# Second products in blocks of seven for two of three token groups, and weight sums made in the first group

## The chip, the core and the metric

The kernel runs on one core of a Trainium2 chip. The core has five engines with queues of their own, each worked through in order: TensorE (PE, matrix products into PSUM), VectorE (DVE), ScalarE (ACT), GpSimd (POOL, cannot reach PSUM) and SyncE (SP), which here issues nearly all DMA transfers. The metric is the device time of one launch in microseconds (us); the kernel before takes 1295.29 us (median of three runs, 1294.5 to 1299.32).

## The reference, cut to what matters

```python
# q, k, v: [4, 8, 576, 64]
attn = softmax(q_c @ k_c.T / sqrt(64)) @ v_c          # in chunks of 64 positions
x = attn, rearranged to [2304, 512]
h = maximum(x @ w_in, 0);  x = h * h @ w_out          # first layer: 512 -> 2048 -> 512
p = domain_probs / (domain_probs.sum(-1, keepdims=True) + 1e-9)
for e in range(4):                                    # second layer: four experts
    h = maximum(x @ w1[e], 0)                         # 512 -> 1024
    out += p[:, e:e+1] * (h @ w2[e])                  # 1024 -> 512
```

All of it is float32. The kernel writes each operand as a high part (rounded for the fast matmul) and a low part (the rest), and makes three matmuls (high-high, high-low, low-high) for each product.

## The kernel before

**First layer.** Attention and the first layer run in ticks r = 0 to 85. The 2304 tokens are five blocks of 384, 384, 512, 512 and 512; the 2048 hidden features are four passes of four groups of 128. So the first layer has 80 steps, 20 in a pass: 8 of 384 tokens and 12 of 512. Step m runs in tick r = m + 5. A tick has twelve matmuls of l1 (first matrix, L298) for step m, then twelve of l2 (second matrix, L331) for step m - 1. Between them ScalarE takes the relu (L309), VectorE squares (L310), ScalarE makes the high part (L314), VectorE the low part (L315); the l2 of the next tick reads these. From tick 22 on attention is over. The first layer's weights come as 64-bit numbers; each of 32 units is converted (unit_convert, unit_split: ScalarE L129, L130, L151, four steps of VectorE, GpSimd L143, L144, L152) in a tick that UOFF and SECOND give: in the third pass at ticks 26, 28, 30, 33 and 41 to 44, in the fourth at 46, 48, 50, 53 and 61 to 64.

**Jobs.** The second layer's products are made with seven block products in place of eight (a Strassen form), which needs sums of weight blocks. A job takes one of 16 pieces (four experts, four chunks of 256 hidden features) of one of the two weights: it loads the blocks (job_load, three DMAs), makes four sums on GpSimd (L470), splits the seven blocks in four parts into high and low (ScalarE L477 for the high part, then GpSimd or VectorE L479 for the low one) and stores them to DRAM (kept, L484). There are 32 jobs, one every second tick from tick 20 on, interleaved with the first layer: loaded in tick r, summed in r + 2, split from half a tick later on. The split tile jsplit has three buffers, jraw three.

**Second layer.** The tokens are three groups of 768 (six tiles of 128: three of a top half, three of a bottom half). Each group has 16 steps, numbered n = 0 to 47 in all. A step has seven slots u. In slot u stands one product of the first kind for step n (c_unit, L529: six matmuls of 384 columns), and, for steps whose first product is finished, three products of the second kind (d_unit, L610: nine matmuls of 256 columns). c_finish turns the first products into the blocks A11, A12, A22 and the sums S1 to S4 (VectorE L547, L541; GpSimd L578; ScalarE L551 and GpSimd L552 split them). d_move takes the second products out of PSUM: B and A collect into the tile uw, O, x1, x0, o1, o0 scale by the probability of the expert and add to the output tile, F adds uw at the end of an expert (j == 3); B at an expert's first step (j == 0) is a copy on ScalarE (L627). At every step w1_load and w2_load bring the stored sums back (1792 KB each). The output has six tiles of one buffer each.

The order on each engine is the order in which this code issues; there is no scheduler.

Of the kernel before, what the change touches and what calls it, by code (L numbers as in the profile page):

```python
# [18 lines left out]
P = 128  # L19
# [17 lines left out]
JOB_AT, JOB_EVERY = 20, 2  # L37
# [7 lines left out]
def tile_kernel(ctx, tc, q, k, v, moe_w_in, moe_w_out, moe2_p, moe2_w1, moe2_w2, out):  # L45
# [395 lines left out]
    def job_load(which, n):  # L441
        e, j = divmod(n, NP)
        r = late["jb"].tile([P, 7, 2 * P], F32, tag="raw", name="jraw", bufs=3)
        if which == 1:
            for i, h0, h1, slot in ((0, 0, 2, 1), (1, 0, 1, 0), (1, 1, 2, 3)):
                f0 = (2 * j + i) * P
                nc.sync.dma_start(
                    out=r[:, slot:slot + h1 - h0].rearrange("p h (k f) -> p (h k) f", k=2),
                    in_=moe2_w1[e, h0 * 2 * P:h1 * 2 * P, f0:f0 + P].rearrange("(k p) f -> p k f", p=P),
                )  # L450
        else:
            f0 = 2 * j * P
# [12 lines left out]
    def job(which, n):

        r = job_load(which, n)
        yield 4
        for o, a, b, op in SUMS[which]:
            nc.gpsimd.tensor_tensor(out=r[:, o], in0=r[:, a], in1=r[:, b], op=op)  # L470
        yield 3
        c = NW // 4
        done = []
        for part in range(4):
            x = r.rearrange("p s c -> p (s c)")[:, part * c:(part + 1) * c]
            w = late["jb"].tile([P, 2, c], F32R, tag="split", name="jsplit", bufs=3)
# [3 lines left out]
            done.append((kept[which, n][:, :, part * c:(part + 1) * c], w.bitcast(F32)))  # L480
# [437 lines left out]
```

## Time and profile before

| | |
|---|---|
| median of three runs | 1295.29 us |
| the profiled execution | 1293.79 us, of which 1292.0 us are the span of the trace |
| TensorE, weight loads | 1217.7 us (94%), 1133.6 us (88%) |
| VectorE, ScalarE, GpSimd | 67%, 50%, 60% busy |
| granted TensorE clock, mean | 0.974 of full speed |

Busy means that an instruction was being executed, at whatever clock; waits are shown beside the instruction that came after them, with what ended them.

### The profile page before, as it was taken

What the parts mean: (1) busy time and instruction counts of PE and PEld (TensorE: products, weight loads), DVE (VectorE), ACT (ScalarE), POOL (GpSimd) and SP (SyncE); (2) the same over time, 40 slices, a digit from 0 to 9 for tenths busy, and PEclk for the clock granted to TensorE, in tenths of its full rate; (3) what the DMA queues carried; (4) which work ended last, traced back from release to release, by engine and by line L of the source; (5) the groups of instructions that cost most, each with busy time, mean ns of one, the idle gap of its engine ahead of it and who ended that gap; (6) DMA issues with size and microseconds to landing.
All of it is one profiled execution on the core that took longest, in us unless ns stands there. A gap on an engine that the chain in (4) does not pass through costs nothing.

```text
span 1292.0 us, 22549 instructions
## 1 busy us (share of the span) xinstructions
PE 1217.7 (94%) x8344; PEld 1133.6 (88%) x8344; DVE 866.3 (67%) x1437; ACT 641.6 (50%) x1335; POOL 773.5 (60%) x773
## 2 busy tenths in 40 slices
PE   7899997898799899989999999999999999999997
PEld 6798886776677788879999999899999989999996
DVE  6965774457655746646767677676767766767676
ACT  5655554444444444544545456545444564545453
POOL 3500278667765865835676668476756675656665
PEclk7999998999999899999999999999999999999999
DMA  9854136685659388586666666766665686666562
GB/s 205 194 119 122 43 91 206 216 289 181 218 197 302 133 290 278 205 330 265 259 256 229 229 239 257 269 263 254 251 228 229 245 302 229 259 263 235 228 229 106
DMA packets 152381, 288.81 MB, mean 224 GB/s; under 512 B 66000, under 2 KB 127440, under 8 KB 146128
## 3 DMA queue, kind: packets, MB, share of 16 engines
q1 hardware_dynamic: 149648, 286.72, 64.0%
q8 instruction: 65, 1.06, 0.3%
q10 hardware_dynamic: 2624, 0.66, 0.2%
q14 instruction: 44, 0.36, 0.1%
HBM read 223.91 MB, written 63.44 MB: 222 GB/s over the span
## 4 chain that ended last, share of the span: by engine, by line
PE 73%; DMA 8%; DVE 6%; ACT 4%; POOL 4%; issue 3%; SPq 2%; DVEq 0%; ACTq 0%; POOLq 0%
PE psa L610 25%; PE pst L529 21%; PE psa L331 10%; PE pst L298 5%; PE psh L298 4%; PE psh L529 4%; DMA w2d<-jsplit 3%; DMA w1d<-jsplit 2%; POOL jsplit L479 2%; DMA q<-in_q 1%; PE pst L274 1%; POOL raw L143 1%; DMA k<-in_k 1%; ACT jsplit L477 1%; PE pst L218 1%
## 5 line engine op out<-in xcount | busy, mean ns | idle before, releaser
L529 PE MATMUL pst<-ar 128*128 128x384 f32 x1728 | 349.1, 337 | 4.6 <-ACT u L559 3.7
L529 PEld LDWEIGHTS pst<-ar 128*128 128x128 f32 x1728 | 291.0, 189 | 5.4 <-ACT u L559 4.1
L331 PE MATMUL psa<-ar 128*128 128x512 f32 (+1 forms) x960 | 238.1, 392 | 37.1 <-ACT ar L314 34.1
L552 POOL TENSOR_TENSOR ar<-s,ar 128x384 fp32r<-128x384 f32 x192 | 194.7, 1025 | 107.0 <-ACT ar L551 102.3
L331 PEld LDWEIGHTS psa<-ar 128*128 128x128 f32 x960 | 182.5, 198 | 73.9 <-ACT ar L314 39.7
L610 PE MATMUL psa<-ar 128*128 128x256 f32 x1512 | 212.7, 284 | 12.4 <-ACT uw L627 8.9
L610 PEld LDWEIGHTS psa<-ar 128*128 128x128 f32 x1512 | 201.0, 188 | 19.5 <-ACT uw L627 12.6
L610 PE MATMUL psa<-w2x,ar 128*128 128x256 f32 x1512 | 202.0, 278 | 0.6 <-DVE uw L629 0.4
L610 PEld LDWEIGHTS psa<-w2x,ar 128*128 128x128 f32 x1512 | 195.7, 188 | 2.3 <-DVE uw L629 0.6
L643 POOL TENSOR_TENSOR o<-o,x 128x256 f32<-128x256 f32 x135 | 106.6, 790 | 100.7 <-ACT x L639 100.6
L551 ACT CAST ar<-s 128x384 fp32r<-128x384 f32 x192 | 98.5, 513 | 91.0 <-DVE s L547 85.9
L631 DVE TENSOR_TENSOR uw<-psa,uw 128x512 f32<-128x512 f32 x144 | 95.1, 687 | 66.7 <-ACT uw L627 31.7
L143 POOL TENSOR_TENSOR raw<-raw 128x512 f32<-128x512 f32 x32 | 35.1, 1098 | 173.5 <-DVE raw L142 84.1
L479 DVE TENSOR_TENSOR jsplit<-jraw,jsplit 128x448 fp32r<-128x448 f32 x64 | 56.4, 881 | 110.1 <-ACT jsplit L477 102.1
L298 PE MATMUL pst<-ar 128*128 128x512 f32 (+1 forms) x576 | 129.7, 375 | 0.0
L477 ACT CAST jsplit<-jraw 128x448 fp32r<-128x448 f32 x128 | 71.0, 567 | 106.7 <-DMA w1d<-jsplit 46.3
L298 PEld LDWEIGHTS pst<-ar 128*128 128x128 f32 x576 | 108.5, 193 | 14.5
L559 ACT COPY u<-pst 128x384 f32<-128x384 f32 x144 | 69.9, 486 | 91.5 <-PE pst L529 88.1
L629 DVE TENSOR_TENSOR uw<-psa,uw 128x512 f32<-128x512 f32 x108 | 74.6, 691 | 55.6 <-PE psa L610 55.2
L479 POOL TENSOR_TENSOR jsplit<-jraw,jsplit 128x448 fp32r<-128x448 f32 x64 | 77.5, 1211 | 56.0 <-ACT jsplit L477 48.4
L570 ACT ACTIVATE ar<-psh 128x384 fp32r<-128x384 f32 x96 | 47.3, 492 | 124.4 <-DVE psh L566 66.2
L470 POOL TENSOR_TENSOR jraw<-jraw 128x256 f32<-128x256 f32 x128 | 105.9, 848 | 2.5
(118 smaller groups left out, 1811.5 us busy)
## 6 DMA issues: line engine op xcount, KB each, us to landing
ar<-w1d SPq DMA_DIRECT2D x48, 1792.0 KB, 7.5
ar<-w2d SPq DMA_DIRECT2D x48, 896.0 KB, 7.8
w2x<-w2d SPq DMA_DIRECT2D x48, 896.0 KB, 7.5
w1d<-jsplit SPq DMA_DIRECT2D x64, 448.0 KB, 3.8
w2d<-jsplit SPq DMA_DIRECT2D x64, 448.0 KB, 3.6
raw<-in_moe_w_in SPq DMA_DIRECT2D x16, 512.0 KB, 5.3
raw<-in_moe_w_out SPq DMA_DIRECT2D x16, 512.0 KB, 5.5
jraw<-in_moe_w SPq DMA_DIRECT2D x32, 256.0 KB, 4.3
```

The costliest lines, as they stand in the source:

```text
L298: nc.tensor.matmul(ph[:, :T], lhsT=w[:, kk, :], rhs=x[tb][:, kk, :], start=(kk == 0 and n == 0), stop=(kk == KD - 1 and n == 2),)
L331: nc.tensor.matmul(o, lhsT=w, rhs=y, start=(f == 0 and n == 0), stop=(f == G - 1 and n == 2))
L470: nc.gpsimd.tensor_tensor(out=r[:, o], in0=r[:, a], in1=r[:, b], op=op)
L477: nc.scalar.copy(w[:, 0], x)
L479: eng.tensor_tensor(out=w[:, 1], in0=x, in1=w[:, 0].bitcast(F32), op=ALU.subtract)
L529: nc.tensor.matmul(p, lhsT=w[:, kk, :], rhs=y[:, kk, :], start=(kk == 0 and z == 0 and u in (0, 1, 3)), stop=(kk == 1 and z == 2 and u in ...
L551: nc.scalar.copy(h, st[n, nm])
L552: nc.gpsimd.tensor_tensor(out=l, in0=st[n, nm], in1=h.bitcast(F32), op=ALU.subtract)
L610: nc.tensor.matmul(p, lhsT=w, rhs=y, start=(k in (1, 7) and z == 0), stop=(k in (3, 4) and z == 2), skip_group_check=True,)
L629: nc.vector.tensor_tensor(out=uw, in0=b, in1=uw, op=ALU.add)
L631: nc.vector.tensor_tensor(out=uw, in0=pb[n, t, 0], in1=uw, op=ALU.add)
L643: nc.gpsimd.tensor_tensor(out=o1[:, :2 * P], in0=o1[:, :2 * P], in1=x, op=ALU.add)
```

## The change

The second products of group 1 (steps n = 0 to 15) are made plainly: plain_unit makes six matmuls of 512 columns for each of the six token tiles, plain_move adds them to the output tile. Groups 2 and 3 keep the seven-block form. The second weight's sums are still made by jobs beside the first layer, 16 of them, in the ticks of the new list JOBS, with jsplit in four buffers and jraw in two. The first weight's sums are made in group 1 itself: w1_raw loads a piece two or three steps ahead, w1_add makes the four sums on GpSimd, w1_split writes high and low parts straight to the place from which the matmuls read, and w1_keep stores them for groups 2 and 3. w2_raw and w2_split bring the plain second weight. What the first two steps need is done in ticks 67 to 81 (early), in a pool that takes the place of the first layer's weight buffers. There are eight output buffers; B of the third tile at j == 0 goes to VectorE; the last step has an order of its own (LAST).

```diff
-JOB_AT, JOB_EVERY = 20, 2
+JOBS = [23, 26, 29, 32, 35, 44, 47, 50, 53, 56, 64, 67, 70, 73, 76, 79]
+SWAP = 67
...
+    def job(n):
...
+        r = late["jb"].tile([P, 7, 2 * P], F32, tag="raw", name="jraw", bufs=2)
...
         yield 4
-        for o, a, b, op in SUMS[which]:
-            nc.gpsimd.tensor_tensor(out=r[:, o], in0=r[:, a], in1=r[:, b], op=op)
-        yield 3
+        for o, a, b in ((4, 0, 1), (5, 3, 4), (0, 0, 3), (6, 2, 5)):
+            nc.gpsimd.tensor_tensor(out=r[:, o], in0=r[:, a], in1=r[:, b], op=ALU.subtract)
+        yield 2
...
-            w = late["jb"].tile([P, 2, c], F32R, tag="split", name="jsplit", bufs=3)
+            w = late["jb"].tile([P, 2, c], F32R, tag="split", name="jsplit", bufs=4)
...
+    def w1_add(n, part):
+        r = raw1[n]
...
+        nc.gpsimd.tensor_tensor(out=r[:, o], in0=r[:, a], in1=r[:, b], op=op)
...
+    def w1_split(n, part):
+        c = NW // 2
+        if part == 0:
+            w1_slot(n)
+        h, l = (y[:, part * c:(part + 1) * c] for y in w1c[n])
+        a = raw1[n].rearrange("p s k f -> p (s k f)")[:, 2 * P + part * c:2 * P + (part + 1) * c]
+        nc.scalar.copy(h, a)
+        nc.gpsimd.tensor_tensor(out=l, in0=a, in1=h.bitcast(F32), op=ALU.subtract)
+
+    def w1_keep(n):
+        nc.sync.dma_start(out=kept[1, n].rearrange("p z c -> p (z c)"), in_=w1_slot(n))
+
+    def w2_split(n, part):
...
+        nc.scalar.copy(h, a)
+        nc.gpsimd.tensor_tensor(out=l, in0=a, in1=h.bitcast(F32), op=ALU.subtract)
...
         elif at == 5:
             nc.vector.tensor_tensor(out=d, in0=d, in1=st[n, "u2"], op=ALU.add)
+            if plain(n):
+                nc.scalar.activation(out=g[n][A21][0], in_=d, func=AF.Relu)
+                return
...
+        elif at == 6 and plain(n):
+            low(n, A21, d)
+            nc.scalar.activation(out=g[n][A12][0], in_=b, func=AF.Relu)
...
+    def plain_unit(n, t):
...
+        for i in range(2):
+            hi, lo = g[n][((A11, A21), (A12, A22))[i][tau]]
+            for z, (w, y) in enumerate(((hi, bh), (hi, bl), (lo, bh))):
+                nc.tensor.matmul(
+                    p, lhsT=w[:, ts], rhs=y[:, i, :], start=(i == 0 and z == 0), stop=(i == 1 and z == 2)
+                )
+
+    def plain_move(n, t):
...
+        if m == 0:
+            nc.scalar.activation(out=o, in_=p, func=AF.Copy, scale=pe)
+        else:
+            nc.vector.scalar_tensor_tensor(out=o, in0=p, scalar=pe, in1=o, op0=ALU.mult, op1=ALU.add)
...
             b = pb[n, t, 1]
-            if j == 0:
+            if j == 0 and t == 2:
+                nc.vector.tensor_copy(out=uw, in_=b)
+            elif j == 0:
                 nc.scalar.copy(uw, b)
...
+    LAST = {
+        1: ((0, "B"),), 2: ((1, "B"),), 3: ((0, "A"), (0, "W"), (1, "A"), (1, "W"), (0, "x1"), (0, "o1")),
+        4: ((0, "F"), (0, "D1"), (1, "x1"), (1, "o1"), (0, "O"), (0, "D0")),
+        5: ((1, "F"), (1, "D1"), (1, "x0"), (1, "o0"), (1, "D0")),
+        6: ((2, "B"), (2, "A"), (2, "W"), (2, "F")), 7: ((2, "X"), (2, "D1"), (2, "O"), (2, "D0")),
+    }
...
+        early = {
+            SWAP: [(w1_raw, (0,)), (w1_raw, (1,)), (w2_raw, (0,))],
+            LEAD + NS - 4: [(w1_split, (0, 0)), (w1_split, (0, 1)), (w1_raw, (2,))],
+        }
...
+                if u in (0, 1) and n + 1 < NU:
+                    w1_split(n + 1, u)
+                if u == 1 and n < NU:
+                    w1_keep(n)
+                    if n + 3 < NU:
+                        w1_raw(n + 3)
+                if u in (2, 3) and n < NU:
+                    w2_split(n, u - 2)
+                if u == 3 and n + 1 < NU:
+                    w2_raw(n + 1)
+                if u >= 3 and n + 2 < NU:
+                    w1_add(n + 2, u - 3)
+                if 0 < n <= NU and u < 6:
+                    t = (u + 3) % 6
+                    plain_unit(n - 1, t)
+                    plain_move(n - 1, t)
```

Where the change moves instructions, the programs of before and after read as follows. First ScalarE in the ticks of the conversion cluster of the third pass (ticks 41 to 43); line numbers of the changed kernel are one higher here, and its job copy is L461. Before:

```order
L314 CAST ar<-pst 128x512
L129 ACTIVATE cv<-raw 128x512
L130 ACTIVATE raw<-raw 128x512
L477 CAST jsplit<-jraw 128x448 x2
L309 ACTIVATE r<-pst 128x512
L314 CAST ar<-pst 128x512
L129 ACTIVATE cv<-raw 128x512
L130 ACTIVATE raw<-raw 128x512
L151 CAST ar<-cv 128x512
L477 CAST jsplit<-jraw 128x448 x2
L309 ACTIVATE r<-pst 128x512
```

and after:

```order
L315 CAST ar<-pst 128x512
L130 ACTIVATE cv<-raw 128x512
L131 ACTIVATE raw<-raw 128x512
L310 ACTIVATE r<-pst 128x512
L315 CAST ar<-pst 128x512
L130 ACTIVATE cv<-raw 128x512
L131 ACTIVATE raw<-raw 128x512
L152 CAST ar<-cv 128x512
L310 ACTIVATE r<-pst 128x512
```

The pair of job copies that stood between the conversion and the relu of the next tick is gone from these ticks.

TensorE where the first layer ends and the second begins (L298 and L331 are l1 and l2, L529 the first product, L610 the second; after: L299, L332, L562, and L674 is plain_unit). Before:

```order
L298 MATMUL psh<-ar 128x512 x12
L331 MATMUL psa<-ar 128x512 x12
L529 MATMUL pst<-ar 128x384 x6
L331 MATMUL psa<-ar 128x512 x12
L529 MATMUL psh<-ar 128x384 x6
L529 MATMUL pst<-ar 128x384 x36
L529 MATMUL psh<-ar 128x384 x6
L610 MATMUL psa<-ar 128x256 x9
```

and after:

```order
L299 MATMUL psh<-ar 128x512 x12
L332 MATMUL psa<-ar 128x512 x12
L562 MATMUL pst<-ar 128x384 x6
L332 MATMUL psa<-ar 128x512 x12
L562 MATMUL psh<-ar 128x384 x6
L562 MATMUL pst<-ar 128x384 x36
L674 MATMUL psa<-ar 128x512 x6
L562 MATMUL psh<-ar 128x384 x6
```

The second product of step 0 begins one slot earlier, and a slot has six matmuls of 512 columns where it had nine of 256.

GpSimd in one step of group 1 (s are the sums S1 to S4, x the scaled products, raw the weight pieces). Before:

```order
L643 TENSOR_TENSOR o<-o,x_5826 128x256
L643 TENSOR_TENSOR o<-o,x_5850 128x256
L578 TENSOR_TENSOR s_5865<-s_5861,a_5768 128x384
L552 TENSOR_TENSOR ar<-s_5863,ar 128x384
L552 TENSOR_TENSOR ar<-s_5865,ar 128x384
L552 TENSOR_TENSOR ar<-s_5861,ar 128x384
L643 TENSOR_TENSOR o<-o,x_5925 128x256
L552 TENSOR_TENSOR ar<-s_5913,ar 128x384
L651 TENSOR_TENSOR o<-o,x_5927 128x512
```

and after, two steps:

```order
L510 TENSOR_TENSOR ar<-raw_5084,ar 128x896 x2
L522 TENSOR_TENSOR ar<-raw_5260,ar 128x512 x2
L496 TENSOR_TENSOR raw_5218<-raw_5218 128x256 x4
L510 TENSOR_TENSOR ar<-raw_5218,ar 128x896 x2
L522 TENSOR_TENSOR ar<-raw_5390,ar 128x512 x2
L496 TENSOR_TENSOR raw_5348<-raw_5348 128x256 x4
```

The splits of sums and the output additions are replaced by the splits and sums of weights; the sums of one step (L496) are read by the splits (L510) of the next.

## Rows read from the trace of the kernel before

**Rows 1.** The page, part 1: busy us, share of the span, instructions.
```profile
PE 1217.7 (94%) x8344; PEld 1133.6 (88%) x8344; DVE 866.3 (67%) x1437; ACT 641.6 (50%) x1335; POOL 773.5 (60%) x773
```

**Rows 2.** Busy time by stretch: start:end, length, each engine's busy us (instructions), PEclk, DMA, GB/s.
```profile
171.28:546.53 375.25, 338.17 (x1513) 287.50 (x1512) 224.53 (x334) 169.33 (x323) 261.66 (x255) 0.95 0.67 222
546.53:563.23 16.70, 12.11 (x56) 10.87 (x54) 8.81 (x15) 6.40 (x13) 4.14 (x3) 0.90 0.80 297
563.23:803.53 240.30, 236.68 (x1671) 234.28 (x1672) 167.42 (x280) 126.47 (x280) 154.90 (x157) 1.00 0.66 252
803.53:1284.20 480.67, 471.25 (x3329) 464.68 (x3327) 340.67 (x564) 244.57 (x546) 306.31 (x317) 1.00 0.64 241
1284.20:1292.00 7.80, 0.00 (x0) 0.00 (x0) 4.09 (x5) 0.69 (x1) 2.75 (x3) 0.62 0.54 202
...
305.00:325.00 20.00, 15.53 (x60) 12.74 (x59) 14.98 (x20) 9.43 (x18) 17.40 (x16) 0.83 0.46 145
...
460.26:546.53 86.27, 86.08 (x409) 74.58 (x409) 52.15 (x76) 41.09 (x77) 57.88 (x57) 1.00 0.76 258
```

**Rows 3.** The chain that ended last, in order of time: start us, us, what.
```profile
466.68 2.08 PE psa L331 x12
...
494.31 2.72 PE psa L331 x12
```

**Rows 4.** Waits of TensorE and ScalarE: who for whom, us in total, times, longest.
```profile
PE psa L331 <- ACT ar L314: 34.1, 16, 4.6
...
ACT jsplit L477 <- DMA w1d<-jsplit: 46.3, 20, 4.8
ACT jsplit L477 <- DMA w2d<-jsplit: 41.0, 22, 4.7
```

**Rows 5.** Timeline of TensorE: start, us, line, operation, count, [idle before, releaser].
```profile
317.21 5.79 PE L331 MATMUL psa<-ar 128*128 128x512 f32 x12 [4.47 <-ACT ar L314]
```

**Rows 6.** Timeline of ScalarE at the same place.
```profile
313.73 0.56 ACT L477 CAST jsplit<-jraw 128x448 fp32r<-128x448 f32 x1 [4.66 <-DMA w2d<-jsplit]
```

**Rows 7.** The page, part 6: DMA issues, KB each, median us to landing.
```profile
ar<-w1d SPq DMA_DIRECT2D x48, 1792.0 KB, 7.5
...
w1d<-jsplit SPq DMA_DIRECT2D x64, 448.0 KB, 3.8
```

**Rows 8.** Groups by line, GpSimd, 171 to 547 us: count, busy us, mean ns, idle before.
```profile
L470 POOL TENSOR_TENSOR jraw<-jraw 128x256 f32<-128x256 f32 x128 | 105.9, 848 | 2.5
...
L479 POOL TENSOR_TENSOR jsplit<-jraw,jsplit 128x448 fp32r<-128x448 f32 x62 | 74.5, 1202 | 52.9 <-ACT jsplit L477 45.9 <-DVE ar L315 4.1 <-DMA w2d<-jsplit 2.9
...
L152 POOL TENSOR_TENSOR ar<-cv,ar 128x512 fp32r<-128x512 f32 x22 | 29.1, 1323 | 3.8 <-ACT ar L151 3.8
...
L144 POOL TENSOR_TENSOR cv<-cv,raw 128x512 f32<-128x512 f32 x20 | 27.7, 1383 | 1.6
L143 POOL TENSOR_TENSOR raw<-raw 128x512 f32<-128x512 f32 x20 | 22.6, 1131 | 52.8 <-issue 27.2 <-ACT r L309 23.3 <-ACT acc L346 2.3
```

**Rows 9.** Timeline of TensorE where the second layer begins.
```profile
555.32 7.06 PE L529 MATMUL pst<-ar 128*128 128x384 f32 x30 [3.73 <-ACT u L559]
...
568.63 1.21 PE L529 MATMUL pst<-ar 128*128 128x384 f32 x6
569.68 1.23 PE L610 MATMUL psa<-ar 128*128 128x256 f32 x9
570.74 1.21 PE L529 MATMUL pst<-ar 128*128 128x384 f32 x6
```

**Rows 10.** Timeline of TensorE: the second first-product group (psh) of four steps.
```profile
805.74 1.21 PE L529 MATMUL psh<-ar 128*128 128x384 f32 x6
...
824.15 1.21 PE L529 MATMUL psh<-ar 128*128 128x384 f32 x6
...
1170.41 1.21 PE L529 MATMUL psh<-ar 128*128 128x384 f32 x6
...
1186.03 1.23 PE L529 MATMUL psh<-ar 128*128 128x384 f32 x6
```

More of the change, by code (lines that the diff above doesn't have):

```diff
@@ L479, in job @@
             eng.tensor_tensor(out=w[:, 1], in0=x, in1=w[:, 0].bitcast(F32), op=ALU.subtract)
-            done.append((kept[which, n][:, :, part * c:(part + 1) * c], w.bitcast(F32)))
+            done.append((kept[2, n][:, :, part * c:(part + 1) * c], w.bitcast(F32)))
             if part % 2:
@@ L486, in job, with w1_raw @@
                 yield 1
+    raw1, raw2 = {}, {}
+    def w1_raw(n):
+        e, j = divmod(n, NP)
+        r = raw1[n] = late["raw"].tile([P, 8, 2, P], F32, tag="raw1", name="raw1", bufs=2)
+        for i, h0, h1, slot in ((0, 0, 2, 1), (1, 0, 1, 0), (1, 1, 2, 3)):
+            f0 = (2 * j + i) * P
+            nc.sync.dma_start(
+                out=r[:, slot:slot + h1 - h0].rearrange("p h k f -> p (h k) f"),
+                in_=moe2_w1[e, h0 * 2 * P:h1 * 2 * P, f0:f0 + P].rearrange("(k p) f -> p k f", p=P),
+            )
@@ new lines, in w2_raw @@
+    def w2_raw(n):
+        e, j = divmod(n, NP)
+        r = raw2[n] = late["raw"].tile([P, 2, DM], F32, tag="raw2", name="raw2", bufs=1)
+        nc.sync.dma_start(
+            out=r, in_=moe2_w2[e, 2 * j * P:2 * (j + 1) * P, :].rearrange("(h p) d -> p h d", p=P)
+        )
+    def w1_add(n, part):
+        r = raw1[n]
+        o, a, b, op = (
+            (4, 0, 3, ALU.add), (5, 4, 1, ALU.subtract), (6, 1, 0, ALU.subtract), (7, 2, 5, ALU.subtract)
+        )[part]
+        nc.gpsimd.tensor_tensor(out=r[:, o], in0=r[:, a], in1=r[:, b], op=op)
@@ L536, in temp, with plain @@
     def temp(nm, w=HALF, bufs=1):
-        return late["s"].tile([P, w], F32, tag=nm, name=nm, bufs=bufs)
+        return late["s" if nm[0] == "u" else "b"].tile([P, w], F32, tag=nm, name=nm, bufs=bufs)
+    def plain(n):
+        return n < NU
     def low(n, i, p):
@@ L582, in c_finish @@
             split(n, S2, "s2")
+        elif plain(n):
+            if at == 7:
+                low(n, A12, b)
         elif at == 7:
@@ L620, in d_move @@
         p0, p1 = (prob[:, r // P, e:e + 1] for r in (r0, r1))
-        o0, o1 = late["o"][:, t, :], late["o"][:, t + 3, :]
+        if (sp, t) not in late["o"]:
+            new_o(sp, t)
+        o0, o1 = late["o"][sp, t], late["o"][sp, t + 3]
         uw = late["uw"][:, t, :]
@@ L796, in tile_kernel @@
             run_all(do(r, "load"))
-            if r >= JOB_AT and r % JOB_EVERY == 0 and work:
-                going.append([2 * r, job(*work.pop(0))])
+            if r in JOBS:
+                going.append([2 * r, job(JOBS.index(r))])
             advance(2 * r)
@@ L824, in tile_kernel @@
             else:
-                if r == LEAD + NS - 10:
-                    w1_load(0)
+                if r == SWAP:
+                    staging.close()
+                    late["raw"] = raw_pool.enter_context(tc.tile_pool(name="raw", bufs=1, reuse_waits="tile"))
+                for fn, args in early.pop(r, ()):
+                    fn(*args)
                 if r > y0_at:
```

108 lines of the change are left out of this document (65 added, 43 removed).

## Prediction

> **What bounds the kernel now.** I read the page's busy times first: TensorE is busy 94% of the span [rows 1]. That figure hides where time goes, so I cut the span at the program's own borders and read busy time and granted clock per stretch [rows 2]. The stretch from 171.28 to 546.53 us is the first layer after attention (ticks 22 to 84). It is 375.25 us long, TensorE is busy in only 338.17 of it, and its clock is 0.95. In the second layer (563.23 to 1284.20 us) it is busy 98% at clock 1.00.
>
> What should the first stretch take? The chain of waits has undisturbed groups of twelve matmuls: 2.72 us for 512 columns, 2.08 us for 384 [rows 3]. Each of the 63 ticks has two groups, one per matrix of the first layer; from the block sizes (8 of 20 ticks have 384 tokens) that is 78 groups of 512 and 48 of 384: 78 x 2.72 + 48 x 2.08 = 312.0 us. So **63.25 us are lost** there. Who ends the waits? ScalarE's L314 (34.1 us, 16 waits), the copy that feeds the next tick's second matrix; and ScalarE itself stands 46.3 + 41.0 us at L477, a weight job's copy, because its buffer is still being stored [rows 4]. One place shows the chain: ScalarE waits 4.66 us for a store at 313.73 and does L309 and L314 behind it; TensorE stands 4.47 us, and its next twelve matmuls take 5.79 us where 2.72 would do, since the granted clock has fallen (mean 0.83 in those 20 us, between its levels of 1.2 and 2.4 GHz) [rows 2, 5, 6]. Waits and slow matmuls after them are the 63 us.
>
> **The change part by part.** *First layer.* Of 32 jobs 16 stay (second weight), one every third tick in place of every second, none in the ticks of the conversion clusters; the split buffers are four, so a pair of copies no longer meets the store issued half a tick before (reuse is now two or more ticks away, a store of this size lands in 3.8 us [rows 7]). On GpSimd a job is 4 x 0.848 + 2 x 1.202 = 5.8 us and a weight conversion 1.13 + 1.38 + 1.32 = 3.8 us [rows 8]. In a pass of 20 ticks (98.6 us of matmuls) that was 10 x 5.8 + 8 x 3.8 = 88 us of GpSimd and is now 5 x 5.8 + 31 = 60 us. The densest part left is ticks 25 to 32 and 45 to 52, eight 384-token ticks of 4.16 us: about 28 of 33 us. There an in-order GpSimd can still hold ScalarE: where a conversion falls one tick before a job's sums, I follow conversion, sums (3.4 us) and copy by hand, with the lengths of [rows 8], to an estimate of 2.8 us late against 1.8 us of slack: a stall of 1 us, at four or five places. So 5 us of the 63.25 remain: **-58 us**. Bounds: 1 us left (the sums are never late) to 20 us (both dense parts keep half of what such ticks lose now). TensorE's queue gains nothing here.
>
> *Entry to the second layer.* 546.53 to 563.23 us is 16.70 us [rows 2]; the work in it is seven first-product groups at 1.05 us [rows 9] and one l2 group of 2.72, 10.1 us. The 3.73 us wait for a ScalarE copy [rows 9] comes behind the job tail, which now ends two ticks earlier (last job at 79, not 82). The first weights are made in place, so no load is awaited. The new w1_split(1) and w2_split(0) stand in ScalarE's queue between the copies; by their order each copy still has a group's time. I leave 1.5 us of the 6.6 lost: **-5 us**, bounds -6 to -2.5.
>
> *Group 1, TensorE.* The 63 matmuls of 256 columns become 36 of 512. First product: 7 x 1.05 = 7.35 us per step. Plain second product: 36 x 2.72/12 = 8.16 us [rows 3]. So 15.51 us a step, 16 steps = 248.2 us. Before, these 16 steps took 240.30 us [rows 2], the waits at the expert borders in them, and one nine-matmul group of 1.06 us [rows 9] was still owed behind them. **+6.8 us.**
>
> Here the twelve-matmul rows of 512 columns give 227 ns a matmul, and that is what I use. The Trainium skill (TensorE: Matmul & The Clock Gate, section Back-to-back issue gap) gives about 131 ns per matmul of 512 columns in a sustained stream; by it group 1 would take about 193 us as an estimate and the kernel some 55 us less than I forecast. The rows of this trace speak against that, so it gets no chance.
>
> *Group 1, the engines beside it.* GpSimd loses the splits of four sums, the S2 sum and the output additions, and gets per step four 256-column sums (0.848), two 896-column subtractions (no more than twice the 448-column one, 2.4) and two of 512 (1.32) [rows 8]: 3.4 + 4.8 + 2.6 = 10.8 us, two more in the four steps that combine the next group's inputs, under 15.5. ScalarE goes from 16 instructions a step to 11, VectorE from 17 to 13, none longer than twice those removed. What TensorE waits for in a step is low(A21): after its first-product group come an add, a relu, one output update and the subtraction; they have one plain group and two first-product groups of time, 3.5 us, and I estimate 2.9 for them. So the cover is there but thin. SyncE: each step's store of the first weight (1792 KB) stands before the raw loads; the load of that size lands in 7.5 us [rows 7], and the slot is written again six groups, 13 us, later. I add **+2 us**, bounds 0 to +8.
>
> *Groups 2 and 3.* Same matmuls. At each expert border a step is longer, worst where a group begins: 18.41 us for 7 x 1.05 + 7 x 1.06 = 14.8 [rows 9, 10], since ScalarE waits for the output store of the tile it is to refill. Eight output buffers remove that one; moving the third B copy to VectorE removes part of the others, but VectorE is late there itself (its F updates). Seven of these excesses (from that at 805.74 to that at 1170.41, 15.62 long) sum to 11.3 us; I count **-8 us**, bounds -11 to -4.
>
> *End.* From TensorE's last matmul 7.80 us remain [rows 2], with ScalarE, GpSimd and three F updates on VectorE ahead of the last store. In the changed order two F updates are done earlier and the last steps stay on VectorE (B, A, F, X, O). **-1.9 us**, bounds -3 to 0.
>
> Sum against the profiled execution, 1293.79 us (span 1292.0 and 1.8 around it): 1293.8 - 58.2 - 5.1 + 6.8 + 2 - 8 - 1.9 = 1229.4 us. The median of the runs lies 1.5 us over that execution: **1231 us**. All lower ends together give 1220, all upper ends 1260.
>
> **The rivals.**
> *The remaining jobs still stall.* Half the first layer's loss, 32 us, stays: 1258 us. For it: in ticks 25 to 32 and 45 to 52 GpSimd is 84% full, and the sums come in its queue behind conversions which wait for VectorE. Against: the stalls I see end at a store (87.3 us of ScalarE's waits), and the stretch from 460 to 546 us with a job every second tick and no conversion has TensorE busy all the time [rows 2].
>
> *TensorE's work alone decides.* The first layer's waits are filled by others (conversion, SyncE's order), nothing is regained but the matmul time of group 1 is paid: 1295.3 + 8.8 = 1304 us. For it: 94% busy [rows 1]. Against: the busy time includes matmuls at half clock, and the named waits. The Trainium skill (Perfetto Trace Analysis, section Identifying the Most-Contended Engine) says to optimise the engine with the highest occupancy first, which here speaks against adding TensorE work; it also warns that matmul busy time misjudges headroom, and the stretches agree with the warning.
>
> *Slower by the stores of the sums.* ScalarE's w1_split of step n+1 overwrites the slot whose store was issued in step n. If that store needs more than its 13 us and some 3 us of slack, ScalarE stands at the head of each step and the PSUM copies behind it hold TensorE. A 448 KB store lands in 3.8 us [rows 7]; four times that is 15.2, just at the point. At 22 us a step would lengthen by 6 us, 15 steps by 90: about 1320 us. It eats the whole gain from 20 us on. Against: the load of the same size takes 7.5 us, and less is moved per step than now.
>
> *It doesn't do what it says.* The freed ticks don't matter since another wait (raw weight loads) ends last: about 1290 us.
>
> **How the numbers follow.** Forecast 0.72, jobs still stall 0.17, TensorE alone 0.04, stores 0.04, no effect 0.03. The range 1218 (the lower ends without the 1.5 us) to 1258 us holds nearly all of the forecast and half of the first rival, near 0.8. A measurement of this kernel tells about 0.5% from no change; faster by more than that 0.91, within it 0.03, slower 0.06.
>
> **What would show it.** In the profile after: ticks 22 to 84 within 332 us, clock 0.99 or more there, ScalarE's waits for jsplit stores gone; group 1 steps of 15.5 to 15.8 us with TensorE busy 98%; GpSimd near 70% in group 1; no wait over 1 us at the group borders. Steps over 17 us in group 1 with ScalarE waiting on w1d stores would make the store rival right; waits of ScalarE on GpSimd's sums in ticks 26 to 35 and 46 to 56 the first.

## The result, and the profile of the changed kernel

The changed kernel takes **1235.65 us** (median of four runs, 1234.67 to 1237.4); the kernel before took 1296.45 us in the runs beside it (1294.5 to 1299.32). The ratio is 0.9531, with a 95% interval of 0.9507 to 0.9554: 4.7% faster. The forecast was 1231 us with a range of 1218 to 1258 us. The profiled execution took 1237.4 us, of which 1235.3 are the span.

The page's first part, as in [rows 1]:

```profile
PE 1203.5 (97%) x7912; PEld 1109.9 (90%) x7912; DVE 797.2 (65%) x1334; ACT 586.3 (47%) x1171; POOL 688.9 (56%) x652
```

TensorE's busy time fell by only 14 us while the span fell by 57: what went is waiting, and matmuls at the lower clock (in ticks 22 to 84 TensorE is busy 317.59 us for the same matmuls that took 338.17 [rows 2]); group 1 has 13.8 us more of busy time. The same borders of the program as in [rows 2] show where (columns as there: start:end, length, busy us of TensorE, weight loads, VectorE, ScalarE, GpSimd, granted clock, DMA share, GB/s). Ticks 22 to 84 are the second row, the entry to the second layer the third, group 1 the fourth, groups 2 and 3 the fifth up to the second product group of the last step, and the end the sixth:

```profile
0.00:173.21 173.21, 157.10 (x1780) 134.17 (x1781) 121.25 (x244) 94.17 (x175) 43.73 (x41) 0.96 0.56 129
173.21:496.44 323.23, 317.59 (x1513) 276.74 (x1512) 198.94 (x305) 142.72 (x266) 181.78 (x172) 0.99 0.47 158
496.44:507.07 10.63, 10.27 (x55) 9.44 (x54) 6.22 (x11) 5.16 (x10) 5.60 (x4) 1.00 0.01 2
507.07:757.51 250.44, 250.44 (x1250) 224.95 (x1249) 129.04 (x208) 103.72 (x186) 153.92 (x124) 1.00 0.56 196
757.51:1203.46 445.95, 444.79 (x3158) 442.46 (x3157) 322.27 (x538) 230.82 (x517) 286.64 (x296) 1.00 0.66 252
1203.46:1235.30 31.84, 23.34 (x164) 22.17 (x162) 19.50 (x33) 9.66 (x21) 17.20 (x19) 0.88 0.30 108
```

The last two stretches of the kernel before, cut at the same places:

```profile
803.53:1260.41 456.88, 448.68 (x3167) 443.30 (x3166) 324.19 (x537) 235.10 (x526) 290.15 (x299) 1.00 0.67 249
1260.41:1292.00 31.59, 22.57 (x164) 21.38 (x162) 20.57 (x32) 10.15 (x22) 18.90 (x20) 0.91 0.30 109
```

Side by side. The nine matmuls of a second product that were owed behind group 1 (1.06 us) stand in the prediction with group 1, so 1.06 us are moved from one row to the other here too.

| stretch | before | after | difference | forecast |
|---|---|---|---|---|
| start to tick 22 | 171.28 | 173.21 | +1.9 | 0 |
| ticks 22 to 84 | 375.25 | 323.23 | -52.0 | -58.2 |
| entry to the second layer | 16.70 | 10.63 | -6.1 | -5.1 |
| group 1 | 240.30 + 1.06 | 250.44 | +9.1 | +6.8 + 2 |
| groups 2 and 3 | 456.88 - 1.06 | 445.95 | -9.9 | -8 |
| the last step's end | 31.59 | 31.84 | +0.25 | -1.9 |
| span | 1292.0 | 1235.3 | -56.7 | -64.4 |

### The profile page after: what moved, and what is told of

The parts are those of the page before. It is cut to its first block, busy times and chain, and to the rows that moved or that the text cites. A ratio compares the mean times of both kernels' runs of the same rounds, so it can differ in the third digit from the quotient of the medians.

```text
span 1235.3 us, 20890 instructions
## 1 busy us (share of the span) xinstructions
PE 1203.5 (97%) x7912; PEld 1109.9 (90%) x7912; DVE 797.2 (65%) x1334; ACT 586.3 (47%) x1171; POOL 688.9 (56%) x652
## 5 line engine op out<-in xcount | busy, mean ns | idle before, releaser
L562 PE MATMUL pst<-ar 128*128 128x384 f32 x1728 | 344.4, 335 | 0.4 <-ACT u L595 0.4
L562 PEld LDWEIGHTS pst<-ar 128*128 128x128 f32 x1728 | 295.7, 188 | 8.0 <-ACT u L595 0.7
L332 PE MATMUL psa<-ar 128*128 128x512 f32 (+1 forms) x960 | 221.1, 373 | 5.6 <-ACT ar L315 4.4
L332 PEld LDWEIGHTS psa<-ar 128*128 128x128 f32 x960 | 174.1, 188 | 32.8 <-ACT ar L315 5.7
L588 POOL TENSOR_TENSOR ar<-s,ar 128x384 fp32r<-128x384 f32 x128 | 129.7, 1025 | 63.6 <-ACT ar L587 61.7
L674 PE MATMUL psa<-ar 128*128 128x512 f32 x576 | 149.0, 394 | 0.0
L657 PE MATMUL psa<-ar 128*128 128x256 f32 x1008 | 140.4, 283 | 1.8 <-DVE uw L706 0.8
L657 PE MATMUL psa<-w2x,ar 128*128 128x256 f32 x1008 | 135.3, 280 | 3.4 <-DVE uw L710 3.4
L657 PEld LDWEIGHTS psa<-w2x,ar 128*128 128x128 f32 x1008 | 131.0, 189 | 4.6 <-DVE uw L710 3.6
L688 DVE SCALAR_TENSOR_TENSOR o<-psa,prob,o 128x512 f32<-128x512 f32 x90 | 67.6, 751 | 94.2 <-PE psa L674 94.1
L299 PE MATMUL pst<-ar 128*128 128x512 f32 (+1 forms) x576 | 127.2, 369 | 0.0
L674 PEld LDWEIGHTS psa<-ar 128*128 128x128 f32 x576 | 106.5, 188 | 16.8 <-DVE ar L577 0.3
L299 PEld LDWEIGHTS pst<-ar 128*128 128x128 f32 x576 | 105.4, 188 | 14.3
L510 POOL TENSOR_TENSOR ar<-raw,ar 128x896 fp32r<-128x896 f32 x32 | 68.0, 2128 | 79.0 <-ACT ar L509 79.0
L724 POOL TENSOR_TENSOR o<-o,x 128x256 f32<-128x256 f32 x89 | 70.4, 791 | 68.5 <-ACT x L720 68.5
L299 PE MATMUL psh<-ar 128*128 128x512 f32 (+1 forms) x384 | 90.5, 379 | 2.2 <-DVE ar L283 2.2
L712 DVE TENSOR_TENSOR uw<-psa,uw 128x512 f32<-128x512 f32 x96 | 63.4, 688 | 30.6 <-PE psa L657 20.6
```

The lines of the kernel that those rows point to most:

```text
L299: nc.tensor.matmul(ph[:, :T], lhsT=w[:, kk, :], rhs=x[tb][:, kk, :], start=(kk == 0 and n == 0), stop=(kk == KD - 1 and n == 2),)
L332: nc.tensor.matmul(o, lhsT=w, rhs=y, start=(f == 0 and n == 0), stop=(f == G - 1 and n == 2))
L510: nc.gpsimd.tensor_tensor(out=l, in0=a, in1=h.bitcast(F32), op=ALU.subtract)
L562: nc.tensor.matmul(p, lhsT=w[:, kk, :], rhs=y[:, kk, :], start=(kk == 0 and z == 0 and u in (0, 1, 3)), stop=(kk == 1 and z == 2 and u in ...
L588: nc.gpsimd.tensor_tensor(out=l, in0=st[n, nm], in1=h.bitcast(F32), op=ALU.subtract)
L657: nc.tensor.matmul(p, lhsT=w, rhs=y, start=(k in (1, 7) and z == 0), stop=(k in (3, 4) and z == 2), skip_group_check=True,)
```

## Experiments: the first layer

The first layer gave nearly all of the gain, and two things were changed there at once: the split buffers (three to four) and the jobs (half as many, every third tick, off the clusters of conversions). Each run below but the last has one time and one profiled execution; the kernel before took 1298.63 us beside the first eight of them. Three of them leave the first layer as it is in the changed kernel, and there the stretch is 323.12, 323.23 and 322.63 us long, so differences of some us are more than the scatter.

**Dense jobs in the changed kernel.**

```diff
-JOBS = [23, 26, 29, 32, 35, 44, 47, 50, 53, 56, 64, 67, 70, 73, 76, 79]
+JOBS = list(range(20, 52, 2))
```

> The changed kernel with its 16 jobs at every second tick from 20 to 50, as densely as the kernel before had them and over the conversions, with four split buffers. Measured: the stretch of ticks 22 to 84 (375.25 us before, 323.23 in the changed kernel, about 313 of matmuls). My theory (with the stores out of the way what is left is GpSimd's queue): in the two stretches of 384-token ticks GpSimd then has 4 jobs x 5.8 + 4 conversions x 3.8 = 38 us in 33 us, so ScalarE waits for sums there: 15 to 25 us lost, first layer 328 to 338, whole kernel 1240 to 1252 us. Rival 'buffers alone': as in the changed kernel, 322 to 325, whole 1235 to 1238. Rival 'place alone': these ticks lose what they lost before (46 us), first layer about 358, whole 1270.

Measured: 1266.15 us. The stretch is 351.63 us long (172.93 to 524.56), 28.4 more than in the changed kernel, with the same work in it. My theory gave 5 to 15 more, "place alone" 35; the second is nearer. But the wait for stores was not gone either (20.5 us of ScalarE's waits): SyncE is one queue in order, and a load for a third job stood in it until a raw buffer was free, with the stores behind it. The waits of SyncE (columns: who for whom, us in total, times, longest) in this run:

```profile
SPq L448 <- POOL jsplit L463: 48.1, 11, 8.3
SPq L448 <- DVE jsplit L463: 24.9, 12, 4.0
```

L448 is a job's load; it stood 73 us in all for readers of the raw buffer.

**The same with three raw buffers.** The room comes from the third buffer of the conversion.

```diff
-CV_BUFS = 3
+CV_BUFS = 2
-JOBS = [23, 26, 29, ...]
+JOBS = list(range(20, 52, 2))
-name="jraw", bufs=2
+name="jraw", bufs=3
```

> The changed kernel with its 16 jobs at every second tick from 20 to 50 (as in the run that took 1266.15 us) but with three raw buffers in place of two, so that job loads do not hold SyncE's queue (there SyncE stood 73 us at job loads for jsplit's readers of the raw buffer; room again from one conversion buffer). If the held queue made that run's loss, first layer falls from 351.6 us to 330 or less, whole kernel to 1236 to 1245. If the density of the jobs over the conversions makes it (GpSimd 38 us of work in 33), it stays at 340 to 352, whole 1254 to 1266. I expect the second.

Measured: 1261.31 us, the stretch 347.19 us. So the held queue was worth some 4.4 us, and the density of the jobs some 24 us. Neither figure is pure: with two conversion buffers ScalarE waits 13.4 us for one of them (L130 for GpSimd's L153), a wait that the run before this one and the changed kernel do not have. No single wait names the loss. The stretch's longest stall, 4.58 us of TensorE, follows a tick in which VectorE had a conversion, the probabilities and a job's subtraction to do, with GpSimd busy beside it. Two of VectorE's rows there (start, us, line, operation):

```profile
340.83 1.55 DVE L463 TENSOR_TENSOR jsplit<-jraw,jsplit 128x448 fp32r<-128x448 f32 x1
342.31 0.55 DVE L311 SCALAR_TENSOR_TENSOR pst<-pst,r 128x384 f32<-128x384 f32 x1
```

L311 is the square on which TensorE's next group depends, and it stands last in that row of work. So there VectorE was late, and no store.

**More split buffers in the kernel before.** First five, with two raw buffers:

```diff
-name="jsplit", bufs=3
+name="jsplit", bufs=5
-name="jraw", bufs=3
+name="jraw", bufs=2
```

> The kernel before, all 32 jobs in their places, with five split buffers in place of three (and two raw buffers in place of three to make the room). Store theory: ScalarE's 87.3 us of waits for stores at L477 go, first layer falls from 375.25 us to 335 or less, whole kernel to about 1256. Load theory (GpSimd, 88 us of work in 98.6 us of matmuls a pass): the waits change their name to GpSimd's sums, first layer 355 to 375, whole 1276 to 1296. I expect between the two, nearer to the first: 345 and 1266.

Measured: 1325.14 us, slower than the kernel before, outside of what either theory gave; the stretch grew to 404.31 us at a mean granted clock of 0.93. The reason is the queue again. First SyncE's longest waits in the stretch, at the job loads L447 and L454; then ScalarE at one place, where the store that it waits for was issued at 321.71 us, behind a load of L454 that went out at 320.37:

```profile
SPq L447 <- DVE jsplit L479: 99.1, 15, 18.0
SPq L454 <- DVE jsplit L479: 84.6, 15, 7.0
```

```profile
325.56 0.56 ACT L477 CAST jsplit<-jraw 128x448 fp32r<-128x448 f32 x1 [6.84 <-DMA w2d<-jsplit]
```

Two raw buffers do not carry three jobs that are under way, so the run said nothing on the split buffers. Therefore once more, with four split buffers and the raw buffers left at three (`CV_BUFS = 2` makes the room):

```diff
-CV_BUFS = 3
+CV_BUFS = 2
-name="jsplit", bufs=3
+name="jsplit", bufs=4
```

> The kernel before with four split buffers in place of three, raw buffers left at three (room comes from a third buffer of the first layer's conversion, two in place of three). In the run with five split and two raw buffers SyncE stood up to 18 us at job loads that waited for a raw buffer, and the stores behind them came late, so it did not test the buffers. Theory 'transfer' (ScalarE waits because a store needs 3.8 us): its 87.3 us of waits at L477 nearly vanish, first layer 335 to 345 in place of 375.25, whole kernel 1254 to 1265 us. Theory 'GpSimd queue' (a store is issued late because L479 stands on GpSimd behind conversions and sums): the waits shrink but return as waits for sums and for stores, first layer 350 to 370, whole 1270 to 1290. I now expect the second: 357 and 1277.

Measured: 1277.36 us, where I expected 1277; the stretch 354.76 us, where I expected 357. The waits for stores that remain there:

```profile
ACT jsplit L477 <- DMA w2d<-jsplit: 13.3, 19, 1.7
ACT jsplit L477 <- DMA w1d<-jsplit: 9.4, 17, 1.5
```

They fell from 87.3 us [rows 4] to 22.7, and only 20.5 of the 63 us came back. (Two conversion buffers cost something of their own, and that is not separated: ScalarE waits 14.5 us for one of them here, L129 for GpSimd's L152, which it does not in the kernel before. So 20.5 us is what the fourth buffer gave less what the third conversion buffer was worth.) The place of [rows 6] in the kernel before shows why a wait "for a store" is not the store's alone. A copy of ScalarE's at 301.84 us needed its low part from GpSimd (L479); there it stood behind the sums of the next job and a conversion, and SyncE issued the stores of the pair when it was done. GpSimd, then SyncE:

```profile
301.33 3.82 POOL L470 TENSOR_TENSOR jraw<-jraw 128x256 f32<-128x256 f32 x4
305.12 1.43 POOL L143 TENSOR_TENSOR raw<-raw 128x512 f32<-128x512 f32 x1
306.63 1.32 POOL L144 TENSOR_TENSOR cv<-cv,raw 128x512 f32<-128x512 f32 x1
307.92 1.47 POOL L152 TENSOR_TENSOR ar<-cv,ar 128x512 fp32r<-128x512 f32 x1
309.36 1.33 POOL L479 TENSOR_TENSOR jsplit<-jraw,jsplit 128x448 fp32r<-128x448 f32 x1
```

```profile
310.71 1.18 SPq L484 DMA_DIRECT2D w2d<-jsplit  x2
```

The low part was begun 7.5 us after its high part. ScalarE stood from 309.07 to 313.73: 1.6 us of that until the stores were issued, and 3.0 us until the buffer was free.

**Three split buffers in the changed kernel.**

```diff
-name="jsplit", bufs=4
+name="jsplit", bufs=3
```

> The changed kernel with three split buffers in place of four, jobs where they are. If the waits for stores made the loss (my theory), the second pair of copies of each job meets the store of the first again: ScalarE stands 2 to 3 us at L461 for w2d stores in most of the 16 jobs (30 to 45 us of its waits), and in the 384-token ticks, with 1.8 us of slack, TensorE stands behind it: first layer 330 to 340 in place of 323.23, whole kernel 1242 to 1252 us. If the lower load of GpSimd and the places make the gain, nothing moves: 322 to 325 and 1234 to 1237.

Measured: 1244.19 us, the stretch 332.18 us, 8.9 more. The waits for w2d stores are back, though with 19.0 us in 8 waits for less than I expected. So the fourth buffer is worth 9 us with the jobs spread and 20 us or more with 32 dense ones. With three buffers, half as many jobs and these spread, 43 of the 63 us are already back.

**The three stalls that were left.** In the changed kernel TensorE waits at three places of the first layer for more than 1 us, each time for the copy L315. One of them on TensorE, ScalarE, GpSimd and VectorE:

```profile
198.59 2.25 PE L299 MATMUL pst<-ar 128*128 128x384 f32 x12
202.37 0.44 PE L332 MATMUL psa<-ar 128*128 128x384 f32 x1 [1.54 <-ACT ar L315]
202.97 3.08 PE L332 MATMUL psa<-ar 128*128 128x384 f32 x11 [0.15 <-DVE ar L316]
```

```profile
198.94 1.03 ACT L461 CAST jsplit<-jraw 128x448 fp32r<-128x448 f32 x2 [2.35 <-POOL jraw L454]
199.88 0.48 ACT L310 ACTIVATE r<-pst 128x384 f32<-128x384 f32 x1
```

```profile
194.13 1.31 POOL L145 TENSOR_TENSOR cv<-cv,raw 128x512 f32<-128x512 f32 x1
195.40 1.30 POOL L153 TENSOR_TENSOR ar<-cv,ar 128x512 fp32r<-128x512 f32 x1
196.65 2.95 POOL L454 TENSOR_TENSOR jraw<-jraw 128x256 f32<-128x256 f32 x4
```

```profile
200.01 1.32 DVE L463 TENSOR_TENSOR jsplit<-jraw,jsplit 128x448 fp32r<-128x448 f32 x1 [5.55 <-ACT jsplit L461]
201.25 0.55 DVE L311 SCALAR_TENSOR_TENSOR pst<-pst,r 128x384 f32<-128x384 f32 x1
```

The sums L454 start when the conversion of the tick ahead is done; ScalarE's L461 waits 2.35 us for them with the relu L310 behind it. One more link follows on VectorE: the job's subtraction L463, released by the same late copy, stands ahead of the square L311, which so starts 0.9 us after the relu is done (199.88 + 0.48), and L315 waits for the square. Moving the jobs off such ticks:

```diff
-JOBS = [23, 26, 29, 32, 35, 44, 47, 50, 53, 56, 64, 67, 70, 73, 76, 79]
+JOBS = [24, 28, 31, 34, 36, 44, 48, 51, 54, 56, 64, 67, 70, 73, 76, 79]
```

> The changed kernel with some jobs moved so that no conversion stands in the tick ahead of a job's sums: ticks 23, 26, 29, 32, 35, 47, 50, 53 become 24, 28, 31, 34, 36, 48, 51, 54. In the changed kernel TensorE waits 1.54, 1.17 and 1.50 us for L315 at 202.37, 232.30 and 320.39 us, and each time matmuls at half clock follow; I read the first two as jobs (23 and 29) whose sums stood on GpSimd behind a conversion of the tick ahead. If that is so, ScalarE's waits for L454 (12.8 us) go to under 3 us and the first layer falls from 323.23 to 316 to 318 us (the third stall, beside the probabilities on VectorE, may stay); whole kernel 1229 to 1231. Rival: the queue of a 384-token tick is full whatever the place, the stalls move with the jobs: 321 to 326, whole 1233 to 1239.

Measured: 1231.44 us, the stretch 317.76 us (-5.5), as expected; the whole kernel is 0.4 us over what I expected. ScalarE's waits for L454 fell from 12.8 to 4.3 us, not to under 3, and the third stall stayed, the one beside the probabilities (1.48 us at 314.48). One thing I had said wrongly: matmuls at half clock followed the first of the three stalls alone (granted clock 1.00 behind the other two). The changed kernel, then this run:

```profile
ACT jsplit L461 <- POOL jraw L454: 12.8, 9, 2.4
```

```profile
ACT jsplit L461 <- POOL jraw L454: 4.3, 4, 1.5
```

## Experiments: the second layer, and all together

**The store twice.**

```diff
         nc.sync.dma_start(out=kept[1, n]..., in_=w1_slot(n))
+        nc.sync.dma_start(out=kept[3, n]..., in_=w1_slot(n))
```

> The changed kernel with the store of the first weight's sums made twice in each step of group 1 (the second time to memory that nobody reads). The rival of the stores said that ScalarE stands at the head of each step if the store needs more than some 16 us. If the changed kernel is near that point, a second store of 1792 KB, which lands after the first, lengthens the 16 steps: 17 us or more in place of 15.64 us, group 1 270 us or more in place of 250.4. If there is room (TensorE is busy for all of group 1 and the store lands in 8.4 us, so two should land in about 17 at worst): ScalarE waits for stores at L509 but TensorE hardly, steps of 15.64 to 16.0, whole kernel 1235 to 1241 us.

Measured: 1236.78 us, group 1 250.44 us long and TensorE busy in all of it, to the hundredth as in the changed kernel. The DMA share rose from 0.56 to 0.81. The two stores in the page's list (KB each, median us from issue to landing):

```profile
w1d<-ar SPq DMA_DIRECT2D x16, 1792.0 KB, 8.5
w3d<-ar SPq DMA_DIRECT2D x16, 1792.0 KB, 12.4
```

The rival of the stores is not near.

**Six output buffers, and the old order at the end.** The two edits act at places far apart, so one run shows both. (Two more lines give the last step the old order; they are left out here.)

```diff
-tag="o", name="o", bufs=8
+tag="o", name="o", bufs=6
...
-for t, what in (AFTER if d < NQ - 1 else LAST).get(at_, ()):
+for t, what in AFTER.get(at_, ()):
```

> The changed kernel with six output buffers in place of eight, and the order of the other steps for the last step too. Places apart, so both are read from one run. Six buffers: if the refill of an output tile made the group borders long (18.41 and 18.18 us before, against 14.88), the border between groups 2 and 3 goes back from 14.88 to about 18 us and the one between 1 and 2 from 14.87 to 16 to 18; if it was the third B on ScalarE, both stay under 15.3. Old order at the end: from the second product group of the last step to the end 31.84 us in the changed kernel, 31.59 before. My reading: the new order lost at TensorE (3.36 us of waiting for VectorE's L710 and a group at half clock) what it won behind TensorE, so the end is 31.5 to 31.9 again. If the new order is better by itself, 33 or more.

Measured: 1234.59 us. The border between groups 1 and 2 is 14.87 us long as in the changed kernel, the one between 2 and 3 15.24 (1009.37 - 994.13) against 14.88. So beside the third B on VectorE the two buffers are worth 0.4 us, not three. The end is 31.33 us, half a microsecond shorter than with the new order, and a little under what I expected.

**Third B on ScalarE again, and another order at the end.**

```diff
-            if j == 0 and t == 2:
-                nc.vector.tensor_copy(out=uw, in_=b)
-            elif j == 0:
+            if j == 0:
                 nc.scalar.copy(uw, b)
...
     LAST = {
-        3: (..., (1, "A"), (1, "W"), (0, "x1"), (0, "o1")),
-        4: ((0, "F"), (0, "D1"), (1, "x1"), (1, "o1"), (0, "O"), (0, "D0")),
-        5: ((1, "F"), (1, "D1"), (1, "x0"), (1, "o0"), (1, "D0")),
-        6: ((2, "B"), (2, "A"), (2, "W"), (2, "F")), 7: ((2, "X"), ...),
+        3: (..., (1, "A"), (0, "x1"), (0, "o1"), (1, "W")),
+        4: ((1, "x1"), (1, "o1"), (0, "O"), (0, "F"), (0, "D1"), (0, "D0")),
+        5: ((1, "x0"), (1, "o0")),
+        6: ((2, "B"), (2, "A"), (2, "W"), (1, "F"), (1, "D1"), (1, "D0")),
+        7: ((2, "F"), (2, "X"), ...),
     }
```

> The changed kernel with the third B copy back on ScalarE, and a new order of the last step: B and A of the third tile go ahead of the second tile's F on VectorE, O of the first tile ahead of its F. Third B on ScalarE: if moving it to VectorE removed most of the excess at the expert borders inside a group (0.6 to 1.9 us each before, 0.05 to 1.4 now), these five steps lengthen by 0.3 to 0.7 us each, about 2.5 us in all, and the group borders stay at 14.9; if the eight buffers did it all, nothing moves. New last step: TensorE's last group no longer waits for VectorE (3.36 us, then half clock), and VectorE's chain of 7.5 us starts at 1222.6 in place of 1224.1: the end takes 29.5 to 30.5 us in place of 31.84. Whole kernel 1235 to 1238 us with both.

Measured: 1236.27 us. The border between groups 2 and 3 is 16.09 us (14.88 in the changed kernel). The six expert borders inside the groups are 15.42, 16.75, 15.82, 15.43, 15.63 and 15.64 us, against 14.93, 16.26, 15.13, 14.94, 15.14 and 15.13: 0.5 to 0.7 us longer each, and back at the lengths of the kernel before (15.43, 16.73, 15.64, 15.43, 15.62 and 15.62). That is 4.4 us in all, where I expected 2.5 and the group borders to stay: the gain at the six inner borders is VectorE's copy, and the buffers have no part in it. The new order made the end 30.27 us in place of 31.84. In the changed kernel TensorE's last group waits for the third tile's B (L710) on VectorE, which stands behind the first two tiles' F (L755, L756) and these behind GpSimd's L724; TensorE and VectorE there:

```profile
1228.31 2.45 PE L657 MATMUL psa<-w2x,ar 128*128 128x256 f32 x9 [3.36 <-DVE uw L710]
```

```profile
1224.14 1.21 DVE L755 SCALAR_TENSOR_TENSOR o<-uw,prob,o 128x512 f32<-128x512 f32 x1 [1.65 <-POOL o L724]
1225.27 0.47 DVE L756 SCALAR_TENSOR_TENSOR o<-uw,prob,o 128x256 f32<-128x256 f32 x1
1225.85 0.75 DVE L738 SCALAR_TENSOR_TENSOR o<-psa,prob,o 128x512 f32<-128x512 f32 x1
1226.52 0.74 DVE L755 SCALAR_TENSOR_TENSOR o<-uw,prob,o 128x512 f32<-128x512 f32 x1
1227.18 0.48 DVE L756 SCALAR_TENSOR_TENSOR o<-uw,prob,o 128x256 f32<-128x256 f32 x1
1227.57 0.68 DVE L710 TENSOR_TENSOR uw<-psa,uw 128x512 f32<-128x512 f32 x1
```

With B and A ahead of the second tile's F the wait is 1.12 us.

**All that helped, in one kernel.** The moved jobs and the last order of the end stand above; beside them:

```diff
-        at(NTILE + 30, "split", probs)
+        at(NTILE + 40, "split", probs)
...
-                if n < NQ and u == 3 and "y" in pend:
+                if n < NQ and u == (3 if n < NU else 5) and "y" in pend:
```

> All that the runs point to, in one kernel: the jobs moved as above; the probabilities made ten ticks later (tick 58, no conversion near); the new order of the last step (30.27 us in place of 31.84); in groups 2 and 3 the combining of the next group's inputs on GpSimd two slots later, since at 883 us it runs beside VectorE's L755 and L756, which then take 1.86 and 0.95 us in place of 0.74 and 0.47, and the step is 16.26 us long in place of 14.88. My sum: first layer 323.23 to 314 (-9), end -1.6, that one step -1.3: 1223 to 1225 us against 1235.65. If the stalls in the first layer move with the jobs, 1232 to 1234.

Measured: **1223.31 us** (five runs, 1222.86 to 1223.53), against 1297.2 us of the kernel before beside it: ratio 0.9433, interval 0.9415 to 0.945. So it beats both kernels. First layer and end:

```profile
171.14:485.68 314.54, 314.18 (x1514) 275.47 (x1513) 198.37 (x305) 142.89 (x266) 183.71 (x172) 1.00 0.48 162
1191.46:1221.70 30.24, 22.48 (x164) 21.29 (x162) 20.10 (x33) 9.66 (x21) 18.22 (x19) 0.91 0.31 114
```

The first layer has 314.54 us where its matmuls need 312; the later probabilities account for the 3.2 us less than with the moved jobs alone, since no other edit of this run acts there. The step that was 16.26 us long is now 15.13 (from 865.81 to 880.94 us), as long as its like in group 3.

## Why the prediction was right, and where it was not

**First layer (-58.2, measured -52.0).** The stretch was the right place, and 63.25 us lost was the right size: the best kernel has 2.5 us of loss in it. Two steps failed. The first is the term of what is left, "a stall of 1 us, at four or five places": 5 us were forecast and 11.2 are left. The mechanism (conversion, sums, copy) was at work at two places, 202.37 and 232.30 us, with VectorE's subtraction as one more link; the third, 320.39 us, has the probabilities on VectorE, which I had not looked at. And a place costs more than its wait: by the starts of TensorE's groups the waits of 1.54, 1.17 and 1.50 us cost 3.8, 1.9 and 2.3 us, 8.0 of the 11.2. The first costs most since the next matmuls ran slower (mean granted clock 0.72 from 202.3 to 206 us, between the levels of 1.2 and 2.4 GHz): three groups of 2.08 us took 10.04, from 198.59 to 208.63. I had seen just that in [rows 5] and left it out of the sum. Slow matmuls do not follow every wait: behind the third one the granted clock stayed at 1.00 here, and was 0.72 in the run with the moved jobs (wait of 1.48 us, next twelve matmuls 3.83 us). What decides that is not settled.

The second is the reason that I set against the first rival: "the stalls I see end at a store". The row named the last link only. The fourth buffer in the kernel before brought back only 20.5 us of the 63 (with a conversion buffer less); at the place of [rows 6] the stores were issued late because GpSimd was late. With half the jobs as well, still dense, the stretch is 347.2 us long; with the same jobs spread it is 323.2. So the place of the jobs was the largest share, 24 us by this pair of runs and 28 by the one with three conversion buffers and the held queue, and I had not priced it by itself. The rival "the remaining jobs still stall" had the right mechanism for about half of those 11 us (moving the jobs gave back 5.5, the later probabilities 3.2), and the sign that I named for it came too: ScalarE waits for the sums in nine of the 16 jobs. Its price of 32 us was too high.

**Entry (-5.1, measured -6.1).** As read: one wait of 0.36 us is left where there were 3.73 [rows 9].

**Group 1 (+8.8, measured +9.1).** The sum was right, its two parts were not. The other engines cost nothing: TensorE is busy for 250.44 of 250.44 us, and the thin cover of low(A21) held. The 2 us that I put there are TensorE's own: a step takes 15.64 us, not 15.51, since six matmuls of 512 columns take 1.38 us, not 1.36. Two groups from the beginning of a step on TensorE:

```profile
510.75 1.55 PE L674 MATMUL psa<-ar 128*128 128x512 f32 x6
512.13 1.21 PE L562 MATMUL pst<-ar 128*128 128x384 f32 x6
```

That is 230 ns per matmul (512.13 - 510.75 over six), where [rows 3] have 227. The 131 ns of the Trainium skill (TensorE: Matmul & The Clock Gate, section Back-to-back issue gap) are not seen here either. GpSimd is 61% busy in group 1 (153.92 of 250.44), not the 70% that I named: the 896-column subtraction takes 2.13 us and a sum 0.74. ScalarE had 17.5 instructions a step before, not 16 (280 in 16 steps [rows 2]), and has 11.6.

**Groups 2 and 3 (-8, measured -9.9).** Right in size, wrong in the share. I gave the group borders to the eight buffers. At the border between groups 2 and 3 six buffers with the copy on VectorE lose 0.4 us, eight with the copy on ScalarE 1.2, and before, with neither, it lost 3.3 (18.18 us, from 1048.58 to 1066.76, against 14.88). So either mends most of it: the harm came from the pair, since ScalarE's copy L627 stood behind ScalarE's own wait for the tile that it was to refill. In the kernel before:

```profile
1061.93 0.47 ACT L639 ACTIVATE o<-psa,prob 128x256 f32<-128x256 f32 x1 [3.17 <-DMA out<-o]
...
1064.57 0.60 ACT L627 COPY uw<-psa 128x512 f32<-128x512 f32 x1
```

The border between groups 1 and 2 (18.41 us in [rows 10], now 14.87) lost nothing in either run; no run has neither edit there, so its 3.5 us may as well come from the plain form of group 1. The six inner borders, some 0.5 us each, are VectorE's copy.

**End (-1.9, measured +0.25).** This step failed. "Two F updates are done earlier" is true, and that was the fault: they went ahead of the copy that TensorE's last group waits for. 3.36 us of waiting and a group in 2.45 us in place of 1.23 ate the 3.3 us that were won behind TensorE (7.80 us [rows 2] to 4.5).

**Start (0, measured +1.9).** Tick 22 begins at 171.28 us before and 173.21 after; in the other runs of the changed kernel and its variants it lies between 170.34 and 173.28. I take it for a difference between executions; its cause is not settled.

**The rivals.** That TensorE's work alone decides is refuted: group 1 cost 9.1 us, and the first layer, the entry and groups 2 and 3 gave back 68. The stores of sums land in 8.4 us, where that rival needed more than 16, and a second store in each step changes nothing. The signs named for the forecast came: the stretch under 332 us (323.2) at clock 0.99, ScalarE's waits for stores gone, steps of 15.64 us. The sign "no wait over 1 us at the group borders" held (0.75 us is the longest in groups 2 and 3 before the end).

## What to carry to other kernels

A row that says "waits for a store" names the last link; ask when the store was issued and what the engine that fills the buffer was doing, before buying buffers. With queues worked through in order, placement can be worth more than buffers (here 24 to 28 us against 9 to 20): spread side work so that no slow chain stands in the queue just ahead of it. Price a stall from the starts of the groups around it, not from its wait alone: slow matmuls can follow. When a last step is reordered, what TensorE still waits for goes first.

## What the runs showed of the hardware that was not expected

VectorE's updates with two inputs in SBUF take longer when a GpSimd instruction that reads SBUF is under way as they start: in the changed kernel L756 takes 0.95 us in place of 0.47 (at 885.45 and 880.09 us), and L755 up to 1.86 in place of 0.74. L755 free, behind the combining of inputs (L385) and ahead of GpSimd's L724, VectorE first, then GpSimd:

```profile
879.43 0.74 DVE L755 SCALAR_TENSOR_TENSOR o<-uw,prob,o 128x512 f32<-128x512 f32 x1
...
883.66 1.86 DVE L755 SCALAR_TENSOR_TENSOR o<-uw,prob,o 128x512 f32<-128x512 f32 x1
...
944.03 0.74 DVE L755 SCALAR_TENSOR_TENSOR o<-uw,prob,o 128x512 f32<-128x512 f32 x1
```

```profile
883.12 1.85 POOL L385 TENSOR_TENSOR acc<-acc,acc 128x768 f32<-128x768 f32 x1
...
944.09 1.27 POOL L724 TENSOR_TENSOR o<-o,x 128x256 f32<-128x256 f32 x1 [0.56 <-ACT x L720]
```

The L755 of 883.66 ends at 885.52, just after GpSimd's L385 (884.97). At 944.03 VectorE is 0.06 us ahead and loses nothing; L724 takes 1.27 us, where most of its kind take 0.74. L738, the same operation and size with one of its inputs in PSUM, takes 0.73 to 0.75 us beside GpSimd too. The Trainium skill (SBUF — State Buffer, section Who interferes with whom) says that a VectorE instruction with two SBUF inputs contends with a GpSimd instruction that reads SBUF; the rows agree. Moving the combining by two slots took 1.1 us out of that step.

The time of a store grows less than its size: 448 KB land in 3.5 us and 1792 KB in 8.4 us, in the changed kernel's page; with a second one right behind it the first still lands in 8.5.
